# Five MLP units inside batch 1's attention chain, its features reordered, its weight loads moved

## The chip, the cores and the metric

One core of a Trainium2 chip. Its engines work side by side, each through its own list of instructions in order: TensorE (PE) does the matrix products, VectorE (DVE) and ScalarE (ACT) the elementwise work and the emptying of PSUM, GpSimd (POOL) small casts and the issue of some DMAs, SyncE (SP) the issue of the other DMAs. They wait for each other through semaphores. The metric is the device time of one execution in microseconds (us), as a median over runs.

## The reference

Eight batches of 576 rows go through an attention with a cosine weighting, without a softmax, and then through a mixer.

```python
def phi(x, c, s):
    r = np.maximum(x, 0.0)
    return np.concatenate([r * c, r * s], axis=-1)
q_p = phi(q, cos_w, sin_w)
k_p = phi(k, cos_w, sin_w)
kv = np.einsum('bhsf,bhsd->bhfd', k_p, v)
z = np.sum(k_p, axis=2)
num = np.einsum('bhsf,bhfd->bhsd', q_p, kv)
den = np.einsum('bhsf,bhf->bhs', q_p, z)[..., None] + 1e-06
...
h = xt @ U @ V
u = x + h.transpose(0, 2, 1)
ch = np.maximum(u @ w_ch1, 0.0) @ w_ch2
return (u + ch).astype(np.float32)
```

There are 8 heads of 64; x has 512 columns, U and V have rank 32, and the hidden layer of the MLP has 2048 columns. All inputs and the output are float32; the kernel multiplies in bf16.

## The kernel before

**Tiles.** A batch's 576 rows are four blocks of 128 (c = 0 to 3) and a tail of 64 (c = 4). ORD = (4, 0, 1, 2, 3) is the order in which they are mostly taken. The tails of an even and an odd batch share one tile of 128 rows.

**Attention of a batch.** q_prep and k_prep (through scaled_relu) make the features: for each block one instruction for the cosine half and one for the sine half, each on the engine that its argument names (V_ is DVE, A_ is ACT, G_ is POOL). qtr_unit transposes a block's q features on PE, eight matmuls, and an engine copies them to q_pT. v_prep and v_block cast v to bf16 in v_ext, with a column of ones. kv_unit makes k times v for four heads, and its last column is z. den_unit forms the denominators and recip their reciprocals; xh_unit forms x of one block for four heads and DVE multiplies it by the reciprocal. A_unit is x U (half the columns at a time here), uTd_open, uTd_mm and uTd_evac (uTd_close is the last two) make the transposed u for the MLP, and u_unit makes the plain u for the final addition: a product with V ("va") on PE and an addition on DVE.

**MLP.** g1_main(b, j) is one unit of the first layer: four matmuls of 512 columns with weights w_ch1, columns 128 j and on, and a ReLU by ACT into hid. g1_tail does the same for a pair's tails, g2_part the second layer and the output. The weights come through POOL's DMA queue in quarters: w1_load(n) serves j = 4n to 4n + 3, w2_load(n) the second layer.

**Order.** Everything is written out by hand. The kernel starts with batch 0's attention (chain_head, chain_mid, chain_end), where keep_warm puts matmuls on zeros between the dependent steps. Then comes a list of slots: for each pair of batches 16 units of the even batch, 16 of the odd, 4 tails, 36 parts of the second layer. After each slot what was put at its number is emitted: `at(j, ...)` for batch 1's attention, `put(...)` for the rest, and attention_plan for batches 2 to 7, whose instructions are put at numbers relative to w.

**Around the change.** Slots 0 to 6 carry batch 1's features and transposes; at slot 7 come the u units of batch 0, then chain_head(1) and chain_mid(1), with unit 8 as its only filling, at slots 9 and 10 the end of the chain. In POOL's queue a one-column copy into mark makes the following weight loads wait until the named tile has landed: before, the first two quarters of w_ch1 behind the first half of v of batch 0, the third and fourth behind the halves of v of batch 1. In SP's queue a small store, mark2, holds back the loads of batch 1 until batch 0's first reciprocals are there, and those of batch 2 until batch 1's second ones. PSUM tiles are named by tag: "g" has three buffers, "o" two, "T" and "X" one each.

Of the kernel before, what the change touches and what calls it, by code (L numbers as in the profile page):

```python
# [17 lines left out]
def kernel(  # L18
# [14 lines left out]
    H = 8  # L33
    S = 576
# [14 lines left out]
    def tail(b):  # L49
        lo = TS * (b % 2)  # L50
        return slice(lo, lo + TS)
# [49 lines left out]
    def cast(eng, o, i):  # L101
        if eng is nc.scalar:
            nc.scalar.activation(out=o, in_=i, func=AF.Copy, bias=0.0, scale=1.0)  # L103
        else:
            eng.tensor_copy(out=o, in_=i)  # L105
# [71 lines left out]
    mark2 = const.tile([1, 1], FP32)  # L177

    def cast_uv():
        cast(A_, U_bf[:, 0:4, 0:R], stU[:, 0:4, :])  # L180
        for i in range(2):
            cast(A_, U_bf[tail(i), 4 + i, 0:R], stU[tail(i), 4, :])
        cast(A_, V_bf[0:R, 0:4, :], stV[:, 0:512].rearrange("r (p c) -> r c p", c=4))
        for i in range(2):
            cast(A_, V_bf[0:R, 4, tail(i)], stV[:, 512:S])


    k_p, q_p, q_pT, kv_sb, x_bf, A_sb = {}, {}, {}, {}, {}, {}
# [2 lines left out]
    def v_prep(b, h0=0, h1=H, cs=range(5), engs=None):  # L191
        vx = v_ext[b % 2]
        for n, c in enumerate(cs):
            eng = engs[n] if engs else G_
            if eng is None:
                continue
            if c < 4:
                cast(eng, vx[:, c, h0:h1, 0:D], vst[b][:, h0:h1, c, :])
            else:
                cast(eng, vx[tail(b), 4, h0:h1, 0:D], vt[b][tail(b), h0:h1, :])  # L200

    def v_block(b, h0, h1, c0, c1, eng):
# [411 lines left out]


    TL = (0, 1, 2, 3, 4)

    def chain_head(b, warm, mid=None):
        v_prep(b, 0, 4, (4,), (A_,))
        v_block(b, 0, 4, 0, 3, V_)  # L620
        v_block(b, 0, 4, 3, 4, A_)
        if mid:
            mid()
        kv_unit(b, 0, "T", 1)
        warm(2, "o", 2)
        rec0 = den_unit(b, 0, 4, "X", 1)
        v_prep(b, 4, 8, (4,), (A_,))
        v_block(b, 4, 8, 0, 4, A_)
        warm(1, "g", 3)
        for n, c in enumerate(ORD):  # L630
            xh_unit(b, c, 0, 4, rec0, *(("o", 2) if n in (0, 1, 4) else ("g", 3)))
            if n == 3:
                kv_unit(b, 1, "T", 1, A_)
        return rec0

    def chain_mid(b, warm, fill):
        warm(1, "g", 3)
        rec1 = den_unit(b, 4, 8, "g", 3)
        if b == 1:

            nc.sync.dma_start(out=mark2, in_=rec1[0:1, 0, 0:1])
        u01 = ps.tile([P, 2, 512], FP32, tag="X", bufs=1, name="u01")
        uTd_open(b, 0, None, None, u01[:, 0, :].rearrange("p (c t) -> p c t", c=4))
        uTd_open(b, 1, None, None, u01[:, 1, :].rearrange("p (c t) -> p c t", c=4))
        a0 = A_unit(b, "T", 1, A_, 0, 256)
        for n, c in enumerate(ORD[:3]):
            xh_unit(b, c, 4, 8, rec1, *(("o", 2), ("g", 3))[n % 2])
        fill()
        uTd_mm(b, 0)
        uTd_mm(b, 1)  # L650
        uTd_evac(b, 0, A_)
        uTd_evac(b, 1, A_)
        for n, c in enumerate(ORD[3:]):
            xh_unit(b, c, 4, 8, rec1, *(("g", 3), ("o", 2))[n % 2])
        return a0

    def chain_end(b, a0):
# [1 line left out]
        uTd_open(b, 2, "o", 2)  # L659
        uTd_open(b, 3, "o", 2)  # L660

    def none(*a):
        pass

    keep_warm(22, "X", 1)
    for c in TL:
        q_prep(0, c, (V_, V_ if c == 3 else A_))
    for n, c in enumerate(TL):
        qtr_unit(0, c, 0, H, (V_, A_, V_, A_, V_)[n], "g", 3)
        keep_warm(1, "o", 2)  # L670
    for c in TL:
        k_prep(0, c, (V_, V_ if c == 3 else A_))
    keep_warm(13, "o", 2)

    def w1_begin():
        G_.tensor_copy(out=mark, in_=vst[0][0:TS, 3, 0, 0:1])
        w1_load(0)
        w1_load(1)

    rec0 = chain_head(0, keep_warm, w1_begin)  # L680
    cast_uv()

    nc.sync.dma_start(out=mark2, in_=rec0[0:1, 0, 0:1])
    alloc_q(1)
# [6 lines left out]
    load_tail(vt[1], v, 1)  # L691
    load_main(vst[1], v, 1, 0, 4)
    load_main(vst[1], v, 1, 4, 8)
    a0 = chain_mid(0, keep_warm, none)
    keep_warm(2, "g", 3)
    chain_end(0, a0)
    g1_main(0, 0, True)
    uTd_close(0, 2, V_)
# [7 lines left out]
    def at(j, *thunks):  # L706
        beside.setdefault(j, []).extend(thunks)

    for n, c in enumerate(ORD):
        at(n, lambda c=c, n=n: q_prep(1, c, (V_, A_ if n % 2 == 0 else V_)))  # L710
        ev = A_ if n == 3 else V_
        tg = ("T", 1) if n % 2 else ("o", 2)
        at(2 + n, lambda c=c, ev=ev, tg=tg: qtr_unit(1, c, eng=ev, tag=tg[0], bufs=tg[1]))
        at((3, 4, 5, 6, 6)[n], lambda c=c, n=n: k_prep(1, c, (V_, A_ if n % 2 else V_)))
    for c in ORD:
        at(7, lambda c=c: u_unit(0, c, "o", 2))

    def w1_end():
        G_.tensor_copy(out=mark, in_=vst[1][0:TS, 3, 0, 0:1])
        w1_load(2)  # L720
        G_.tensor_copy(out=mark, in_=vst[1][0:TS, 7, 0, 0:1])
        w1_load(3)
        for n in range(4):
            w2_load(n)

    at(7, lambda: chain_head(1, none, w1_end))
    st1 = {}
    at(7, lambda: st1.update(a=chain_mid(1, none, lambda: g1_main(0, 8))))
    at(9, lambda: chain_end(1, st1["a"]))
    at(10, lambda: uTd_close(1, 2, V_), lambda: uTd_close(1, 3, A_))  # L730

    slots, todo = [], {}
    for pr in range(NPAIR):
        e, o = 2 * pr, 2 * pr + 1
        slots += [
            (lambda: None) if (pr, j) == (0, 8) else lambda j=j, e=e: g1_main(e, j)
            for j in range(NJ)
        ]
        slots += [lambda j=j, o=o: g1_main(o, j) for j in range(NJ)]
        slots += [lambda j=j, pr=pr: g1_tail(pr, j) for j in range(4)]  # L740
        slots += [
            lambda cc=cc, p=p, pr=pr: g2_part(pr, cc, p) for cc in range(9) for p in range(4)
        ]
# [4 lines left out]
        todo.setdefault(at, []).append(thunk)  # L748

    put(17, lambda: uTt_direct(0, "o", 2, V_))  # L750
    for n, c in enumerate(ORD):
        put(18 + n, lambda c=c: u_unit(1, c, *spare(18)))
    for n, t in enumerate(loads(2, nc.sync)):
        put((11, 12, 12)[n], t)
    for b, w in ((2, 40), (3, 57), (4, 88), (5, 124), (6, 160), (7, 196)):
# [36 lines left out]
```

## Time and profile before

| what | value |
|---|---|
| median of 8 runs | 341.98 us (341.26 to 343.4) |
| the profiled execution | 342.84 us, span 341.1 us |
| mean granted clock of PE | 0.979 of full |
| PE busy | 322.6 us, 95% of the span |
| DVE, ACT, POOL busy | 45%, 49%, 8% |
| q, k of batch 1 (main part) issued, landed | 18.25 to 27.9 us, 20.18 to 32.7 us |
| v of batch 1, both halves landed | 35.1 and 36.1 us |
| third and fourth quarter of w_ch1 landed | 41.0 and 44.5 us |

A landing here is the start of the DMA's issue plus the time to landing that the trace gives. The span runs from the first to the last instruction; the 1.74 us between it and the execution's time lie around it. A row of the timeline gives start, duration, engine, line, instruction and, in brackets, how long the engine stood idle before it and what ended that. A row of the windows gives for each stretch the busy time of the engines, the granted clock of PE, the mean share of the DMA engines, and GB/s. "PEclk" in the page gives the clock in tenths for 40 equal slices of 8.5 us.

### The profile page before, as it was taken

What the parts mean: (1) busy time and instruction counts of PE and PEld (TensorE: products, weight loads), DVE (VectorE), ACT (ScalarE), POOL (GpSimd) and SP (SyncE); (2) the same over time, 40 slices, a digit from 0 to 9 for tenths busy, and PEclk for the clock granted to TensorE, in tenths of its full rate; (3) what the DMA queues carried; (4) which work ended last, traced back from release to release, by engine and by line L of the source; (5) the groups of instructions that cost most, each with busy time, mean ns of one, the idle gap of its engine ahead of it and who ended that gap; (6) DMA issues with size and microseconds to landing.
All of it is one profiled execution on the core that took longest, in us unless ns stands there. A gap on an engine that the chain in (4) does not pass through costs nothing.

```text
span 341.1 us, 5844 instructions
## 1 busy us (share of the span) xinstructions
PE 322.6 (95%) x2428; PEld 172.9 (51%) x2428; DVE 152.1 (45%) x334; ACT 165.5 (49%) x278; POOL 28.3 (8%) x55
## 2 busy tenths in 40 slices
PE   8996679999989979999999999999999999999995
PEld 3663275447545534455645544557445444464444
DVE  7663953381465785034553790144725630001211
ACT  4754805578671904655760376565910046660000
POOL 1200600300101010000011110000011100000000
PEclk9997958999999999999999999999999999999999
DMA  7999799946633412893259939920392140001131
GB/s 237 227 242 262 112 193 294 352 139 213 218 116 124 121 62 63 186 310 107 63 152 270 321 98 218 325 84 2 95 231 59 62 112 2 0 2 62 62 94 62
DMA packets 79054, 50.73 MB, mean 149 GB/s; under 512 B 47188, under 2 KB 76244, under 8 KB 79028
## 3 DMA queue, kind: packets, MB, share of 16 engines
q1 hardware_dynamic: 72596, 39.09, 40.5%
q0 software_dynamic: 6432, 11.27, 13.5%
q8 instruction: 19, 0.31, 0.4%
q14 instruction: 7, 0.06, 0.1%
HBM read 36.86 MB, written 9.44 MB: 136 GB/s over the span
## 4 chain that ended last, share of the span: by engine, by line
PE 64%; DVE 4%; issue 1%; ACT 1%; DVEq 0%
PE o_ps L518 29%; PE g_ps L466 24%; PE gt_ps L486 3%; PE va_ps L382 2%; PE kv_ps L245 2%; PE x_ps L339 2%; DVE k_p L213 2%; PE a_ps L365 2%; DVE o_sb L528 1%; PE t_ps L262 1%; DVE k_tl L213 1%; DVE rec L297 0%; ACT k_p L211 0%; DVE x_bf L349 0%; DVE rec L296 0%
## 5 line engine op out<-in xcount | busy, mean ns | idle before, releaser
L466 PE MATMUL g_ps<-uT,w_bf 128*128 128x512 bf16 x512 | 119.7, 384 | 0.0
L518 PE MATMUL o_ps<-w_bf,hid 128*128 128x512 bf16 (+1 forms) x528 | 118.2, 372 | 0.5 <-DVE o_sb L528 0.5
L475 ACT ACTIVATE hid<-g_ps 128x512 bf16<-128x512 f32 x128 | 76.2, 596 | 83.9 <-PE g_ps L466 83.9
L466 PEld LDWEIGHTS <-w_bf 128*128 128x128 bf16 x512 | 49.1, 99 | 55.7 <-issue 1.7
L518 PEld LDWEIGHTS <-hid 128*128 128x128 bf16 x528 | 49.9, 98 | 53.6 <-issue 1.6
L528 DVE TENSOR_TENSOR o_sb<-u_bf,o_ps 128x512 f32<-128x512 bf16 (+1 forms) x33 | 22.1, 669 | 67.8 <-PE o_ps L518 67.7
L538 POOL DMA_DIRECT2D out_dram<-o_sb x24 | 13.4, 558 | 181.6 <-DVE o_sb L528 164.5
L383 DVE TENSOR_TENSOR u_bf<-x_bf,va_ps 128x512 bf16<-128x512 bf16 x32 | 21.6, 685 | 9.0 <-PE va_ps L382 9.0
L105 DVE CAST kv<-kv_ps 128x260 bf16<-128x260 f32 x14 | 6.0, 428 | 37.7 <-PE kv_ps L245 37.7
L211 ACT ACTIVATE q_p<-qst,sinw 128x512 bf16<-128x512 f32 x29 | 20.4, 709 | 3.8 <-DMA qst<-in_q_dram 3.8
L382 PE MATMUL va_ps<-A_sb,V_bf 128*128 128x512 bf16 x40 | 15.1, 379 | 2.5 <-DVE u_tl L383 1.6
L349 DVE TENSOR_TENSOR x_bf<-x_ps,rec 128x512 bf16<-128x512 f32 x24 | 16.6, 691 | 0.8
L103 ACT ACTIVATE v_ext<-vst 128x512 bf16<-128x512 f32 (+2 forms) x24 | 15.2, 643 | 2.4 <-DMA vst<-in_v_dram 2.3
L486 PE MATMUL gt_ps<-uT_tl,w_bf 128*128 128x128 bf16 x256 | 16.1, 219 | 0.0
L486 PEld LDWEIGHTS <-w_bf 128*128 128x128 bf16 x256 | 15.1, 98 | 1.4
L518 PE MATMUL o_ps<-w_bf,hid_tl 128*128 128x512 bf16 x64 | 15.4, 379 | 0.0
L245 PEld LDWEIGHTS <-k_p 128*128 128x128 bf16 x256 | 12.0, 102 | 5.9 <-DVE v_ext L105 2.2
L172 PE MATMUL w_ps<-zero 128*128 128x512 bf16 x46 | 13.8, 437 | 1.2 <-DVE halfpi L142 1.2
L245 PE MATMUL kv_ps<-v_ext,k_p 128*128 128x65 bf16 x256 | 12.8, 199 | 1.8 <-DVE v_ext L105 1.3
L213 DVE TENSOR_SCALAR k_p<-kst,cosw 128x512 bf16<-128x512 f32 x28 | 13.4, 489 | 0.0
L262 PE MATMUL t_ps<-ident,q_p 128*128 128x128 bf16 x128 | 10.2, 225 | 3.3 <-ACT q_tlT L103 1.6
L339 PEld LDWEIGHTS <-q_pT 128*128 128x128 bf16 x192 | 9.1, 98 | 8.2 <-DVE x_bf L349 1.6
(99 smaller groups left out, 262.1 us busy)
## 6 DMA issues: line engine op xcount, KB each, us to landing
qst<-in_q_dram SPq DMA_DIRECT2D x8, 1024.0 KB, 8.5
kst<-in_k_dram SPq DMA_DIRECT2D x8, 1024.0 KB, 7.9
vst<-in_v_dram SPq DMA_DIRECT2D x6, 1024.0 KB, 9.0
out_dram<-o_sb POOLq DMA_DIRECT2D x24, 256.0 KB, 2.7
w_bf<-in_moe_w_ch_dram POOLq DMA_DIRECT2D x8, 512.0 KB, 9.0
vst<-in_v_dram SPq DMA_DIRECT2D x4, 512.0 KB, 7.0
out_dram<-o_sb SPq DMA_DIRECT2D x7, 256.0 KB, 2.3
qt<-in_q_dram SPq DMA_DIRECT2D x8, 128.0 KB, 7.9
```

Source lines behind the costliest of these rows:

```text
L211: nc.scalar.activation(out=o, in_=i, func=AF.Relu, bias=0.0, scale=w)
L213: eng.tensor_scalar(out=o, in0=i, scalar1=0.0, scalar2=w, op0=ALU.max, op1=ALU.mult)
L245: nc.tensor.matmul(out=acc[:, i, :], lhsT=k_p[b][:, c, h, :] if c < 4 else k_tl[:, h, :], rhs=vx[:, c, h, :], start=(c == 0), stop=(c == 4),)
L339: nc.tensor.matmul(out=acc[:, g, i * E : i * E + E], lhsT=qT_of(b, c, h), rhs=kv_sb[b][:, h, :], start=True, stop=True,)
L349: nc.vector.tensor_tensor(out=x_of(b, c, rows).rearrange("p (g i d) -> p g i d", g=2, d=D), in0=view[:, :, :, 0:D], in1=rec[rows].unsqueez ...
L382: nc.tensor.matmul(out=va, lhsT=V_bf[:, c, :], rhs=A_sb[b], start=True, stop=True)
L383: nc.vector.tensor_tensor(out=u_bf[b][:, c, :] if c < 4 else u_tl[b // 2][rows, :], in0=x_of(b, c, rows), in1=va[rows, :], op=ALU.add,)
L466: nc.tensor.matmul(out=g_ps.rearrange("p (c t) -> p c t", c=4), lhsT=w1_bf[:, d, j * P : j * P + P], rhs=uT[b][:, :, d, :], start=(d == 0) ...
L475: nc.scalar.activation(out=hid[b][:, j, :], in_=g_ps, func=AF.Relu, bias=0.0, scale=1.0)
L486: nc.tensor.matmul(out=g_ps[:, jj, :], lhsT=w1_bf[:, d, j * P : j * P + P], rhs=uT_tl[pr][:, d, :], start=(d == 0), stop=(d == 3),)
L518: nc.tensor.matmul(out=o[:, cols], lhsT=lhs[:, j, c * P : c * P + P], rhs=w2_bf[:, j, cols], start=(j == 0), stop=(j == NJ - 1),)
L528: nc.vector.tensor_tensor(out=o_sb[:, cols], in0=u[:, cols], in1=o[:, cols], op=ALU.add)
```

## The change

The casts of U and V go from ACT to POOL and are emitted before batch 0's chain. POOL's first mark copies from k's tail instead of v; the first quarter of w_ch1 follows it, the second comes behind the casts. The third and fourth and w_ch2 wait for batch 1's k instead of its v. Batch 1's k features come after all its q features, all with cosine on DVE and sine on ACT. Batch 0's u units move from slot 7 to slots 18 to 22, batch 1's to 23 to 27. The chain of batch 1 is emitted whole at slot 7, and units 8 to 12 are put inside it by fill1; their own slots are empty. Two x blocks instead of three come before the second group of uTd steps, and stand ahead of the opens. Batch 0's chain gets the same order with its keep-warm counts in warm0 (seven matmuls where there were six), and batch 1's first v casts go to DVE alone. The u opening of the last two columns is closed at slot 13 instead of 10. What is computed is the same.

```diff
     def cast_uv():
-        cast(A_, U_bf[:, 0:4, 0:R], stU[:, 0:4, :])
+        cast(G_, U_bf[:, 0:4, 0:R], stU[:, 0:4, :])
...
+    O2, G3 = ("o", 2), ("g", 3)
+
+    def chain_head(b, fill, xt, engs):
+        v_prep(b, 0, 4, (4,), (engs[0],))
         v_block(b, 0, 4, 0, 3, V_)
-        v_block(b, 0, 4, 3, 4, A_)
-        if mid:
-            mid()
+        v_block(b, 0, 4, 3, 4, engs[0])
         kv_unit(b, 0, "T", 1)
-        warm(2, "o", 2)
+        fill(0)
         rec0 = den_unit(b, 0, 4, "X", 1)
         v_prep(b, 4, 8, (4,), (A_,))
         v_block(b, 4, 8, 0, 4, A_)
-        warm(1, "g", 3)
+        fill(1)
         for n, c in enumerate(ORD):
-            xh_unit(b, c, 0, 4, rec0, *(("o", 2) if n in (0, 1, 4) else ("g", 3)))
+            xh_unit(b, c, 0, 4, rec0, *xt[n])
+            if n == 1:
+                fill(2)
             if n == 3:
                 kv_unit(b, 1, "T", 1, A_)
         return rec0
 
-    def chain_mid(b, warm, fill):
-        warm(1, "g", 3)
-        rec1 = den_unit(b, 4, 8, "g", 3)
+    def chain_mid(b, fill, xt, dt):
+        fill(3)
+        rec1 = den_unit(b, 4, 8, *dt)
...
+        for n, c in enumerate(ORD[:2]):
+            xh_unit(b, c, 4, 8, rec1, *xt[n])
         u01 = ps.tile([P, 2, 512], FP32, tag="X", bufs=1, name="u01")
...
         a0 = A_unit(b, "T", 1, A_, 0, 256)
-        for n, c in enumerate(ORD[:3]):
-            xh_unit(b, c, 4, 8, rec1, *(("o", 2), ("g", 3))[n % 2])
-        fill()
+        fill(4)
         uTd_mm(b, 0)
         uTd_mm(b, 1)
         uTd_evac(b, 0, A_)
         uTd_evac(b, 1, A_)
-        for n, c in enumerate(ORD[3:]):
-            xh_unit(b, c, 4, 8, rec1, *(("g", 3), ("o", 2))[n % 2])
+        for n, c in enumerate(ORD[2:]):
+            xh_unit(b, c, 4, 8, rec1, *xt[2 + n])
+        fill(5)
         return a0
...
+    def warm0(n):
+        m = (2, 1, 0, 1, 1, 2)[n]
+        if m:
+            keep_warm(m, *(O2 if n == 0 else G3))
...
-    def w1_begin():
-        G_.tensor_copy(out=mark, in_=vst[0][0:TS, 3, 0, 0:1])
-        w1_load(0)
-        w1_load(1)
-
-    rec0 = chain_head(0, keep_warm, w1_begin)
+    G_.tensor_copy(out=mark, in_=kt[0][0:TS, 0, 0:1])
+    w1_load(0)
     cast_uv()
+    rec0 = chain_head(0, warm0, (O2, O2, G3, G3, O2), (A_,))
+    w1_load(1)
...
         at(n, lambda c=c, n=n: q_prep(1, c, (V_, A_ if n % 2 == 0 else V_)))
-        ev = A_ if n == 3 else V_
-        tg = ("T", 1) if n % 2 else ("o", 2)
-        at(2 + n, lambda c=c, ev=ev, tg=tg: qtr_unit(1, c, eng=ev, tag=tg[0], bufs=tg[1]))
-        at((3, 4, 5, 6, 6)[n], lambda c=c, n=n: k_prep(1, c, (V_, A_ if n % 2 else V_)))
-    for c in ORD:
-        at(7, lambda c=c: u_unit(0, c, "o", 2))
-
-    def w1_end():
-        G_.tensor_copy(out=mark, in_=vst[1][0:TS, 3, 0, 0:1])
-        w1_load(2)
-        G_.tensor_copy(out=mark, in_=vst[1][0:TS, 7, 0, 0:1])
-        w1_load(3)
-        for n in range(4):
-            w2_load(n)
-
-    at(7, lambda: chain_head(1, none, w1_end))
+        tg = ("T", 1) if n % 2 else O2
+        at(2 + n, lambda c=c, tg=tg: qtr_unit(1, c, eng=V_, tag=tg[0], bufs=tg[1]))
+        at((6, 6, 7, 7, 7)[n], lambda c=c, n=n: k_prep(1, c, (V_, A_)))
+    at(6, lambda: G_.tensor_copy(out=mark, in_=kst[1][0:TS, 0, 0:1, 0]))
+    at(6, lambda: [w1_load(2), w1_load(3)] + [w2_load(n) for n in range(4)])
     st1 = {}
-    at(7, lambda: st1.update(a=chain_mid(1, none, lambda: g1_main(0, 8))))
-    at(9, lambda: chain_end(1, st1["a"]))
-    at(10, lambda: uTd_close(1, 2, V_), lambda: uTd_close(1, 3, A_))
+
+    def fill1(n):
+        if n > 0:
+            g1_main(0, 7 + n)
+
+    xt1 = (O2, O2, O2, O2, O2)
+    at(7, lambda: chain_head(1, fill1, xt1, (V_,)))
+    at(7, lambda: st1.update(a=chain_mid(1, fill1, xt1, ("T", 1))))
+    at(7, lambda: chain_end(1, st1["a"]))
+    at(13, lambda: uTd_close(1, 2, V_), lambda: uTd_close(1, 3, A_))
...
-            (lambda: None) if (pr, j) == (0, 8) else lambda j=j, e=e: g1_main(e, j)
+            (lambda: None) if pr == 0 and 8 <= j < 13 else lambda j=j, e=e: g1_main(e, j)
...
-    for n, c in enumerate(ORD):
-        put(18 + n, lambda c=c: u_unit(1, c, *spare(18)))
+    for n, (b, c) in enumerate([(b, c) for b in range(2) for c in ORD]):
+        put(18 + n, lambda b=b, c=c: u_unit(b, c, *spare(18)))
```

More of the change, by code (lines that the diff above doesn't have):

```diff
@@ L179, in cast_uv @@
     def cast_uv():
-        cast(A_, U_bf[:, 0:4, 0:R], stU[:, 0:4, :])
+        cast(G_, U_bf[:, 0:4, 0:R], stU[:, 0:4, :])
         for i in range(2):
-            cast(A_, U_bf[tail(i), 4 + i, 0:R], stU[tail(i), 4, :])
-        cast(A_, V_bf[0:R, 0:4, :], stV[:, 0:512].rearrange("r (p c) -> r c p", c=4))
+            cast(G_, U_bf[tail(i), 4 + i, 0:R], stU[tail(i), 4, :])
+        cast(G_, V_bf[0:R, 0:4, :], stV[:, 0:512].rearrange("r (p c) -> r c p", c=4))
         for i in range(2):
-            cast(A_, V_bf[0:R, 4, tail(i)], stV[:, 512:S])
+            cast(G_, V_bf[0:R, 4, tail(i)], stV[:, 512:S])
     k_p, q_p, q_pT, kv_sb, x_bf, A_sb = {}, {}, {}, {}, {}, {}
@@ L616 @@
     TL = (0, 1, 2, 3, 4)
-    def chain_head(b, warm, mid=None):
-        v_prep(b, 0, 4, (4,), (A_,))
+    O2, G3 = ("o", 2), ("g", 3)
+    def chain_head(b, fill, xt, engs):
+        v_prep(b, 0, 4, (4,), (engs[0],))
         v_block(b, 0, 4, 0, 3, V_)
-        v_block(b, 0, 4, 3, 4, A_)
-        if mid:
-            mid()
+        v_block(b, 0, 4, 3, 4, engs[0])
         kv_unit(b, 0, "T", 1)
-        warm(2, "o", 2)
+        fill(0)
         rec0 = den_unit(b, 0, 4, "X", 1)
@@ L660, in chain_end @@
         uTd_open(b, 3, "o", 2)
-    def none(*a):
-        pass
+    def warm0(n):
+        m = (2, 1, 0, 1, 1, 2)[n]
+        if m:
+            keep_warm(m, *(O2 if n == 0 else G3))
     keep_warm(22, "X", 1)
@@ L668 @@
     for n, c in enumerate(TL):
-        qtr_unit(0, c, 0, H, (V_, A_, V_, A_, V_)[n], "g", 3)
-        keep_warm(1, "o", 2)
+        qtr_unit(0, c, 0, H, (V_, A_, V_, A_, V_)[n], *(G3 if n < 3 else O2))
+        keep_warm(1, "X", 1)
     for c in TL:
@@ L693 @@
     load_main(vst[1], v, 1, 4, 8)
-    a0 = chain_mid(0, keep_warm, none)
-    keep_warm(2, "g", 3)
+    a0 = chain_mid(0, warm0, (O2, G3, O2, G3, O2), G3)
     chain_end(0, a0)
```

## The prediction

> **What bounds the kernel now.** I read the page first (busy shares and the 40 slices), then TensorE's timeline from 0 to 130 us, then the table of 2 us windows for the start, then the list of waits and the DMA issues with their landings, and last ScalarE's and VectorE's timelines between 26 and 46 us.
>
> ```profile
> PE 322.6 (95%) x2428; PEld 172.9 (51%) x2428; DVE 152.1 (45%) x334; ACT 165.5 (49%) x278; POOL 28.3 (8%) x55
> ...
> PEclk9997958999999999999999999999999999999999
> ```
>
> TensorE (PE) is the bound. Its granted clock is low in three slices only, all in the first 55 us, and there its busy time is inflated by the half clock. From 60 us on it stands idle for some 5 us before the last instructions. So what the change can win lies between 24 and 64 us. PE's timeline there:
>
> ```profile
> 24.03 2.32 PE L466 MATMUL g_ps<-uT,w_bf 128*128 128x512 bf16 x10
> ...
> 29.12 0.62 PE L262 MATMUL t_ps<-ident,q_tl 128*128 128x128 bf16 x8 [2.77 <-ACT q_tl L211]
> ...
> 40.95 0.38 PE L382 MATMUL va_ps<-A_sb,V_bf 128*128 128x512 bf16 x1 [1.65 <-DVE u_tl L383]
> ...
> 43.82 0.40 PE L245 MATMUL kv_ps<-v_ext,k_p 128*128 128x65 bf16 x4 [1.30 <-DVE v_ext L105]
> ...
> 57.35 6.21 PE L466 MATMUL g_ps<-uT,w_bf 128*128 128x512 bf16 x28
> ```
>
> The bracket is idle time before the row. PE waits for q of batch 1 until 29.12, starves between 38.8 and 43.8 while DVE works through its queue, and then runs the chain of batch 1 (kv at 43.82 to the last close at 57.35) with three MLP units in it. The windows show at what clock (columns: PE, PEld, DVE, ACT, POOL busy, clock, DMA share, GB/s):
>
> ```profile
> 18.00:20.00 2.00, 1.86 (x44) 1.56 (x41) 1.69 (x6) 1.74 (x5) 0.00 (x0) 1.00 1.24 207
> ...
> 30.00:32.00 2.00, 2.00 (x12) 1.16 (x11) 0.59 (x2) 1.44 (x3) 0.00 (x0) 0.50 1.07 232
> ...
> 38.00:40.00 2.00, 1.17 (x5) 0.37 (x4) 2.00 (x4) 1.74 (x4) 2.00 (x3) 1.00 1.22 205
> 40.00:42.00 2.00, 0.75 (x2) 0.19 (x2) 2.00 (x4) 1.59 (x3) 0.81 (x2) 1.00 1.11 148
> 42.00:44.00 2.00, 0.56 (x5) 0.19 (x5) 1.76 (x4) 0.00 (x0) 0.00 (x0) 0.82 1.16 172
> ...
> 46.00:48.00 2.00, 2.00 (x46) 2.00 (x44) 1.50 (x5) 0.00 (x0) 0.00 (x0) 0.50 1.22 197
> ...
> 52.00:54.00 2.00, 2.00 (x8) 0.72 (x7) 0.80 (x3) 0.28 (x1) 0.00 (x0) 0.62 1.24 207
> ```
>
> Two cold stretches: 29.7 to 33.0 after the first gap, 43.4 to 53.5 after the second. DVE is the engine at 2.00 of 2.00 in the second gap. The list of waits (total, times, longest):
>
> ```profile
> POOL mark L719 <- DMA vst<-in_v_dram: 19.8, 1, 19.8
> ...
> DVE k_tl L213 <- DMA kt<-in_k_dram: 2.5, 1, 2.5
> ```
>
> The second is DVE's strict order at work: k's tail lands at 33.06 us, and the eviction of q's transposes stands behind it; the first is what the third weight quarter waits for.
>
> [...] (29.7 to 33.0 is 3.3 us, 43.4 to 53.5 three such windows)[...] 46 to 50 us, full by the profile but with 65-column matmuls, did not restore it. [...] q of batch 1 is issued on SP at 18.25, yet the rate stays at the weights' 200 or so (the first window row above, and finer ones) until 21.0, and only then climbs to over 300. [...] Here POOL issues weights at 37.7 to 40.8 and two k features on DVE take 0.78 and 0.82 us, not 0.48; the other ones beside POOL's issues took 0.47.
>
> **The change part by part.** Prices from the trace, start to start: an MLP unit (4 matmuls) 0.86 us warm, 1.65 cold; 8 transposes 0.45 and 0.85; kv 0.60 and 1.07; den 0.50; xh 0.13; two opens 0.45 and 0.81; half an A_unit 0.54 and 1.06; two uTd_mm 0.43; a va matmul 0.21. DVE feature 0.40, ScalarE feature 0.62, hid 0.5, q_pT eviction 0.6, xh eviction 0.35 to 0.43.
>
> Start (0 to 26 us). POOL's mark waits for k's tail (some 11 us) instead of v's half (12.79), so the first weight quarter is issued 1.5 us sooner; issue to first bytes took 2.2 us before (13.07 to 15.3), so it starts at about 13.5, as v's traffic ends (13.7). Then POOL casts U and V: U's last tail lands near 15.0, six casts make about 1.7 (V's largest between POOL's 0.61 us for 128x512 and ScalarE's 1.13 for this very cast; I take 0.9), and the second quarter is issued at about 16.7 instead of 14.1, ahead of q's issue at 18.25. Its bytes run 18.9 to 21.5 (2.6 us each, as before), so q starts when it did. ScalarE loses 2.1 us of casts (18.51 to 20.5), hidden before because A_unit ended only at 20.3. Warm matmuls go from 6 to 7 in the chain of batch 0: +0.2, against the 0.23 idle at 20.92. Sum 0; bounds -0.7 (q sooner) and +1.0 (U, V or v's second half held up).
>
> q then k (26 to 40 us). PE ends its half units at 26.3 and waits for q to 29.12 as before, and is cold from 29.7 to 33.0. It then issues transposes and units in turn with nothing of k before them on DVE: transpose 29.12 to 29.57, unit to 31.2, to 32.05, unit to 33.4, then warm 33.85, 34.7, 35.15, 36.0, 36.45, and g1 unit 7 at 37.3. DVE (q 7 x 0.40, evictions 0.35 + 4 x 0.6) keeps ahead. k landed at 33.06, hidden. k's five ScalarE features are behind unit 6's and unit 7's evictions: 36.0 + 0.5 + 2 x 0.62 + 0.5 + 3 x 0.62 = 40.1, so kv starts at 40.25. DVE has k and v's first half done at about 39.5. What is late next is thus ScalarE, where before it was DVE. kv starts 3.6 us sooner: the u units (5 x 0.65 on DVE) no longer stand before v_ext, and three k features left DVE.
>
> The chain (40 to 56 us). PE was idle 37.3 to 40.25, so a second cold stretch is likely. At full clock the chain with five units, by the prices: kv 0.6, wait for its eviction 0.5, den 0.5, units 8 and 9 1.73, five xh 0.65, kv 0.6, unit 10 0.86, den 0.5, two xh and opens 0.7, A half 0.54, unit 11 0.86, uTd_mm 0.43, three xh and a wait for their two buffers 0.7, unit 12 0.86, A half and opens 1.0, unit 13 0.86, closes 0.43: 12.3 us. Cold for two windows (39.8 to 46.6, the grid of the old trace), kv ends at 41.3, den runs 42.05 to 42.6, unit 8 to 44.3, two xh and unit 9 to 46.45, and the rest warm to 55.3: 15.05. Before, the same work (units to 13 and the closes) was done at 57.35 + 3 x 0.864 = 59.94. The units' weights: the third quarter is issued at 33.3, on k's landing at 32.7, lands 5.6 us later at 38.9, and is needed at 42.6; the fourth lands near 42, needed near 52. v's traffic ended at 34.3, a microsecond before the weights' first bytes. POOL's issue of six quarters now stands beside DVE's k features: at 0.8 instead of 0.47 five of them end 1.7 us later, of which 0.7 is slack, so kv would be 1.0 late; below zero it can't go, and I take zero, as most such rows took 0.47.
>
> Moved u units. Ten, in slots 18 to 27, each 0.21 on PE beside a 0.86 unit with a 0.69 addition on DVE: five more cost +1.08. DVE then gets batch 2's features up to 4 us late; they had ended at 76.1 for transposes to 86, so that hides. Batch 2's loads start when the weights end (54.3 before, some 51 after), so DMA follows.
>
> Sum. Same cold stretches: 59.94 - 55.3 - 1.08 = 3.5 us. Without the first one PE and so kv come 1.8 us sooner; without the second 2.6: 5.4, 6.1 or 8.0. [...] I take 5.3 as the middle of the mixed cases. The profiled execution is 342.84 (span 341.1 and 1.74 around it), and so 337.5; the median of the runs, 341.98, is 0.86 lower[...]. I keep 337.5, leaving that 0.86 for stalls the walk misses.
>
> **The rivals.** (1) Warm throughout: the units inside the chain and a shorter gap keep the clock; 342.84 - 8.0 = 334.8. For it: the chain of batch 0, with warm matmuls, held 1.00. Against: two idle times of 2.8 us stay. (2) Cold through three windows as before: unit work at 1.65; another 2.5 us lost, gain 1.0, 341.8. For it: 46 to 50 us. Against: with units the array has wider matmuls. (3) Slower: the second weight quarter, now issued just ahead of q, loses the race and waits behind q, k and v, whose traffic ends at 34.3; it lands near 37.5. Unit 4 needs it at 32. PE then finishes units 4 to 7 and three transposes (4.8, plus 1.7 cold) at 44.0, k's features end at 46.4, and the chain and u units at 46.4 + 15.05 + 1.1 = 62.5, 2.6 behind: 345.4. It decides from a landing at about 34.9, where the 3.5 are gone. For it: q got no visible bytes while weights moved. Against: an output store of POOL issued at 92.36 into a load landed in 5.7 us, against 2.7 in the median, so it isn't shut out.
>
> **How the numbers follow.** Forecast (335.5 to 339.5) 0.57; warm 0.14; cold 0.13, half of it within 0.3%; slower 0.12; a hidden gain (DMA or later stages take it back) 0.04. 0.3%, about 1.0 us, is what this kernel's measurement can tell. Faster 0.77, same 0.10, slower 0.13. The range, 334.3 to 342.0, leaves out the slower case and half of the warm one.
>
> **What would show it.** kv of batch 1 near 40 us instead of 43.82, ended by ScalarE; va rows gone from 38 to 42; units 8 to 12 between kv and the closes; the last close near 53 to 55; PEclk 1.0 sooner than 53.5; third quarter issued near 33. Wrong if unit 4 waits for weights, if v lands later than 38, if the gap before kv stays near 5 us, or if the clock stays at 0.5 past 50 us.

## The result, and the profile after

The changed kernel takes 338.09 us, the median of 21 runs (336.28 to 340.21), against 341.95 for the kernel before (58 runs, 339.36 to 343.79): a ratio of 0.9891 with a 95% interval of 0.9874 to 0.9908. The forecast was 337.5. The profiled execution took 337.85 (span 336.1) against 342.84 (span 341.1).

The page of the kernel after, busy shares and the clock in 40 slices:

```profile
PE 319.5 (95%) x2429; PEld 171.2 (51%) x2429; DVE 152.5 (45%) x334; ACT 164.1 (49%) x272; POOL 29.5 (9%) x60
...
PEclk9999879999999999999999999999999999999999
```

One stretch of low clock is left where there were two (slices 5 and 6, about 39 to 46 us), 6.83 us of clock 0.50 in place of 3.41 and 10.24, and TensorE's busy time fell by 3.1 us though it runs one matmul more: what went is matmul time at half clock. The timeline of TensorE after, from 25 to 58 us (start, length, operation; in brackets the idle time ahead of it and who ended it):

```profile
25.02 2.32 PE L466 MATMUL g_ps<-uT,w_bf 128*128 128x512 bf16 x10
28.79 0.62 PE L262 MATMUL t_ps<-ident,q_tl 128*128 128x128 bf16 x8 [1.45 <-ACT q_tl L211]
...
34.49 1.03 PE L466 MATMUL g_ps<-uT,w_bf 128*128 128x512 bf16 x4
38.24 0.25 PE L245 MATMUL kv_ps<-v_ext,k_p 128*128 128x65 bf16 x3 [2.73 <-DVE v_ext L105]
38.70 0.20 PE L245 MATMUL kv_ps<-v_ext,k_p 128*128 128x65 bf16 x1 [0.21 <-ACT k_p L211]
...
40.45 1.87 PE L466 MATMUL g_ps<-uT,w_bf 128*128 128x512 bf16 x4
...
42.55 1.90 PE L466 MATMUL g_ps<-uT,w_bf 128*128 128x512 bf16 x4
...
54.10 3.62 PE L466 MATMUL g_ps<-uT,w_bf 128*128 128x512 bf16 x16
```

The wait for q is 1.45 us instead of 2.77. The va rows that stood between 38 and 42 are gone, unit 7 (the row at 34.49) is followed by a single wait of 2.73, and kv of batch 1 starts at 38.24 instead of 43.82. That wait is ended by VectorE's last cast of v; ScalarE's last k features come 0.5 later, so both engines hold kv at nearly the same time. The closes are done at 54.10; the same work (units to 13 and closes) was done at 59.94 before. The shift stays to the end: the first transposes of batch 2 stand at 72.25 instead of 77.02, 4.8 sooner, and the span is 5.0 shorter. No later stage took any of it back.

The 2 us windows of the kernel after (columns as in the prediction: busy time of PE, PEld, DVE, ACT and POOL, clock, DMA share, GB/s):

```profile
38.00:40.00 2.00, 1.03 (x24) 0.84 (x25) 0.73 (x3) 1.95 (x4) 0.00 (x0) 0.85 1.19 185
40.00:42.00 2.00, 2.00 (x24) 1.00 (x24) 0.46 (x2) 0.19 (x1) 0.00 (x0) 0.50 1.20 187
...
44.00:46.00 2.00, 2.00 (x35) 1.76 (x33) 0.76 (x2) 0.60 (x1) 0.00 (x0) 0.50 1.24 203
46.00:48.00 2.00, 2.00 (x41) 1.45 (x39) 0.73 (x3) 0.98 (x2) 0.00 (x0) 0.94 1.24 208
```

The cold stretch starts at 39.4, after the wait has ended, and lasts until 46.2. That is 6.83 us, twice the 3.41 of the first cold stretch of the kernel before; 3.41 us is called a window here. How many are lost differs from one execution to the next, and the mean clock of each says by how much: one window of 3.4 us at half clock costs 3.4 / (2 x 337) = 0.5% of it. Of 22 executions of the kernel after, ten had 0.984 (three windows, mean 339.5 us), eight 0.989 or 0.990 (two, 337.6), four 0.993 or 0.995 (about one, 336.7). So a window more or less is worth 1 to 2 us (0.9 and 1.9 between these classes), and the median of a version depends on how often it falls into each class.

### The profile page after: what moved, and what is told of

Read it like the earlier page. It is cut to its first block, busy times and chain, and to the rows that moved or that the text cites. A ratio compares the mean times of both kernels' runs of the same rounds, so it can differ in the third digit from the quotient of the medians.

```text
span 336.1 us, 5849 instructions
## 1 busy us (share of the span) xinstructions
PE 319.5 (95%) x2429; PEld 171.2 (51%) x2429; DVE 152.5 (45%) x334; ACT 164.1 (49%) x272; POOL 29.5 (9%) x60
## 4 chain that ended last, share of the span: by engine, by line
PE 65%; DVE 4%; issue 1%; ACT 1%; DVEq 0%
PE o_ps L518 30%; PE g_ps L466 25%; PE gt_ps L486 3%; PE va_ps L382 2%; PE kv_ps L245 2%; PE x_ps L339 2%; DVE k_p L213 2%; PE a_ps L365 2%; DVE o_sb L528 1%; PE t_ps L262 1%; DVE k_tl L213 1%; DVE rec L297 0%; ACT k_p L211 0%; DVE x_bf L349 0%; DVE rec L296 0%
## 5 line engine op out<-in xcount | busy, mean ns | idle before, releaser
L172 PE MATMUL w_ps<-zero 128*128 128x512 bf16 x47 | 14.1, 430 | 1.4 <-DVE halfpi L142 1.2
L296 DVE TENSOR_SCALAR rec<-x_ps 128x8 f32<-128x8 f32 (+1 forms) x30 | 4.9, 165 | 17.0 <-PE x_ps L339 16.9
```

## The experiments

Each ratio is to the kernel before, run on the same chip beside it, with its 95% interval; that kernel's medians there were 341.25, 341.03 and 341.39 in the three groups of four. The diffs are against the kernel after unless something else is said.

### What held kv: the u units on VectorE's queue

**u_back** puts batch 0's u units back ahead of batch 1's chain.

```diff
+    for c in ORD:
+        at(7, lambda c=c: u_unit(0, c, *O2))
     at(7, lambda: chain_head(1, fill1, xt1, (V_,)))
...
-    for n, (b, c) in enumerate([(b, c) for b in range(2) for c in ORD]):
-        put(18 + n, lambda b=b, c=c: u_unit(b, c, *spare(18)))
+    for n, c in enumerate(ORD):
+        put(18 + n, lambda c=c: u_unit(1, c, *spare(18)))
```

> The changed kernel with one part undone: batch 0's u units stand before batch 1's chain again. Theory (DVE's order sets the start of kv): five additions of 0.65 us stand before DVE's v casts, which end at 38.1 in the changed kernel, so kv of batch 1 starts 3.0 to 3.3 us later, near 41.5; the five va matmuls (1.08) are then paid inside the wait, so 2.0 to 2.3 us slower than the changed kernel, ratio to before 0.995 to 0.997. Rival (ScalarE's k features, which end at 38.65, hold kv anyway and hide DVE): less than 0.5 us slower, ratio 0.989 to 0.991.

Measured: 338.81 us, 0.9939 (0.9906 to 0.9972). TensorE's timeline of u_back:

```profile
36.90 0.38 PE L382 MATMUL va_ps<-A_sb,V_bf 128*128 128x512 bf16 x1 [1.53 <-DVE u_tl L383]
...
40.38 0.42 PE L245 MATMUL kv_ps<-v_ext,k_p 128*128 128x65 bf16 x4 [1.70 <-DVE v_ext L105]
```

The va rows wait again for VectorE's additions, and kv starts 5.94 us after the end of unit 7 (34.44), against 2.89 after 35.35 in the kernel after. That is 3.05 us for five additions and their va matmuls, the size that was expected for kv. The whole lost less than expected: 0.995 to 0.997 was said, and by the two ratios it is some 1.6 us slower than the kernel after instead of 2.0 to 2.3.

**only_u** is the reverse: the kernel before with nothing changed but that move.

```diff
-    for c in ORD:
-        at(7, lambda c=c: u_unit(0, c, "o", 2))
...
-    for n, c in enumerate(ORD):
-        put(18 + n, lambda c=c: u_unit(1, c, *spare(18)))
+    for n, (b, c) in enumerate([(b, c) for b in range(2) for c in ORD]):
+        put(18 + n, lambda b=b, c=c: u_unit(b, c, *spare(18)))
```

> The kernel before with one part alone: batch 0's u units moved from slot 7 to slots 18 to 22, batch 1's to 23 to 27. Theory: five additions of 0.65 us leave DVE's queue before its v cast, kv of batch 1 starts about 3 us sooner (near 40.8 on the old trace), and 1.1 us of va matmuls come later: 1.5 to 2.0 us faster than before, ratio 0.994 to 0.996. Rival (PE's wait only moves, ScalarE's v casts end at 40.1 and 41.6 anyway): ratio 0.998 to 1.000.

Measured: 337.97 us, 0.9912 (0.9877 to 0.9947), so 3.0 us by this move alone where 1.5 to 2.0 were expected. TensorE's timeline of only_u:

```profile
29.89 1.03 PE L262 MATMUL t_ps<-ident,q_tl 128*128 128x128 bf16 x8 [3.47 <-ACT q_tl L211]
...
41.16 0.30 PE L245 MATMUL kv_ps<-v_ext,k_p 128*128 128x65 bf16 x4 [2.24 <-DVE v_ext L105]
...
53.95 6.21 PE L466 MATMUL g_ps<-uT,w_bf 128*128 128x512 bf16 x28
```

Everything up to q is as in the kernel before (the wait is even 3.47), and yet kv starts at 41.16, 2.7 sooner (3.4, counted from the first transposes), and the long run of units at 53.95 instead of 57.35. Its executions spread from 0.980 to 1.000 in clock, two of eight without any cold window (336.3); in the execution shown the clock fell both after the wait for q and in the chain. This one move has most of the change's gain: 0.0088 of the 0.0109 in ratio (0.0053 to 0.0123 by its interval).

### The units inside the chain

**no_fill** takes all five out of the chain and runs them behind it; **fill3** keeps three units ahead of the closes, all late as in the kernel before: two inside the chain (8 and 9, in its last two places for a unit) and the third, unit 10, in its own slot.

```diff
     def fill1(n):
-        if n > 0:
-            g1_main(0, 7 + n)
+        if n > 3:
+            g1_main(0, 4 + n)
...
-    at(13, lambda: uTd_close(1, 2, V_), lambda: uTd_close(1, 3, A_))
+    at(10, lambda: uTd_close(1, 2, V_), lambda: uTd_close(1, 3, A_))
...
-            (lambda: None) if pr == 0 and 8 <= j < 13 else lambda j=j, e=e: g1_main(e, j)
+            (lambda: None) if pr == 0 and 8 <= j < 10 else lambda j=j, e=e: g1_main(e, j)
```

(This is fill3. In no_fill, fill1 returns at once, and slots 8 to 12 run their units.)

> The changed kernel with one part undone: no MLP unit inside batch 1's chain, units 8 to 12 run after it. Theory (the units cover waits[...]): the chain's own waits (for DVE's and ScalarE's evictions) are bare and its clock stays low, 1.0 to 3.0 us slower than the changed kernel, ratio 0.992 to 0.998; kv starts at the same 38.2. Rival (PE's work is the same, so where the units stand is without effect): within 0.5 us, ratio 0.988 to 0.991.

> The changed kernel with three units beside batch 1's chain instead of five, standing late as in the kernel before: unit 8 in the middle, unit 9 before the last A half, unit 10 before the closes. The move of the u units alone gave 0.991, the whole change 0.989, no unit at all 0.999. Theory (the first waits of the chain, at den and xh, are bare again and the clock stays low there): 0.5 to 1.5 us slower than the changed kernel, ratio 0.990 to 0.994. Rival (the first two units carry the effect): as without units, ratio 0.996 or more. Second rival (three are enough): 0.989 or less.

Measured: no_fill 340.87 us, 0.9991 (0.9972 to 1.001); fill3 338.83, 0.9909 (0.9884 to 0.9934). TensorE's timeline of no_fill:

```profile
37.43 0.40 PE L245 MATMUL kv_ps<-v_ext,k_p 128*128 128x65 bf16 x4 [3.03 <-DVE v_ext L105]
...
41.01 0.83 PE L321 MATMUL xh_ps<-kv,q_pT 128*128 128x64 bf16 x8 [0.66 <-DVE x_tl L325]
...
46.93 0.86 PE L431 MATMUL u<-V_bf,A_sb 128*128 128x512 bf16 x2 [0.48 <-ACT A_sb L103]
```

With no units the whole gain is gone, more than the 0.992 to 0.998 that was expected, although kv starts at 37.43. The chain then shows six waits (0.52, 0.66, 0.26, 0.48, 0.39, 0.19) and stays cold (clock 0.50) from 37.2 to 47.5; the executions lie between 0.973 and 0.985. But fill3, with the first group of steps bare as it was before (waits of 0.52, 0.66 and 0.26), is slower than the kernel after by 0.2% in ratio, and the intervals overlap: that units stand in the chain matters, while five instead of three can't be told from no gain. Set beside only_u, fill3 says more: it is the whole change but for where the units stand, and its 0.9909 is only_u's 0.9912. With late units, the new start, the order of q and k and the earlier weights together show no gain of their own.

### The clock

**warm_gap** fills the wait in front of kv with twelve matmuls on zeros, which are the kernel's own keep-warm; **warm4** with four.

```diff
+    at(7, lambda: keep_warm(12, "X", 1))
     at(7, lambda: chain_head(1, fill1, xt1, (V_,)))
```

> The changed kernel with twelve matmuls on zeros (2.6 us warm) put into PE's wait before kv of batch 1 (35.4 to 38.2). Theory (the wait is what makes the clock low from 39.4 to 46): the chain runs at full clock, 2.5 to 3.0 us faster where two cold windows followed, about 2 us on the median, ratio 0.982 to 0.986, mean clock 0.995 or more. Rival (the chain's own narrow matmuls make the clock fall): no gain, ratio 0.988 to 0.992, with 0.5 again behind kv.

> The changed kernel with four matmuls on zeros (0.9 us) before kv instead of twelve, so that about 2 us of the wait stay idle. Theory [...] the clock falls in some executions or none, mean clock above the changed kernel's: ratio 0.980 to 0.987. Rival (any wait of 2 us before narrow matmuls makes it fall): clock 0.984 to 0.990 as without zeros, ratio 0.988 or more.

Measured: warm_gap 333.77 us, 0.9802 (0.9757 to 0.9846), somewhat more than was expected; warm4 335.39, 0.9811 (0.9767 to 0.9856), as its theory had it. The timeline of warm_gap, and its windows:

```profile
33.88 2.75 PE L172 MATMUL w_ps<-zero 128*128 128x512 bf16 x12
...
38.44 0.54 PE L304 MATMUL d_ps<-kv,q_pT 128*128 128x1 bf16 x16 [0.52 <-DVE kv L105]
...
49.90 3.62 PE L466 MATMUL g_ps<-uT,w_bf 128*128 128x512 bf16 x16
```

```profile
42.00:44.00 2.00, 2.00 (x44) 1.53 (x41) 0.88 (x3) 0.97 (x2) 0.00 (x0) 1.00 1.24 204
```

The clock is 1.000 in five of six executions, and the closes are done 11.5 us after den starts (14.2 in the kernel after). By the ratios that is 3.0 us below the kernel after (4.3 between the medians, but the kernel before ran 0.7 faster beside warm_gap), by work that computes nothing. With four zeros a wait of 2.17 stays:

```profile
37.01 0.36 PE L245 MATMUL kv_ps<-v_ext,k_p 128*128 128x65 bf16 x4 [2.17 <-DVE v_ext L105]
```

(TensorE's timeline of warm4.) Its profiled execution was at full clock, like one other (mean 333.7); the other four had 0.990 to 0.994 and took 335.2 to 336.5. So with four zeros it differs from one execution to the next whether a window is lost; what decides it isn't shown.

**no_fill_warm** joins no_fill and the twelve zeros, to see whether the units do more than keep the clock.

```diff
     def fill1(n):
-        if n > 0:
-            g1_main(0, 7 + n)
+        return
...
+    at(7, lambda: keep_warm(12, "X", 1))
```

> Units 8 to 12 out of batch 1's chain, as in the run without them, and twelve matmuls on zeros in the wait before kv, as in the run with them. If the units were worth 3.4 us because they keep the clock up, the zeros do that too: clock 0.995 or more and ratio near 0.986, half or more of the loss gone. If they were worth it because they cover the chain's own waits, most of the 3.4 us stays: ratio 0.989 or more against the 0.980 of the run with zeros and units. If the chain's narrow matmuls make the clock fall whatever stands before it: 0.5 within the chain again, ratio 0.995 or more.

Measured: 338.9 us, 0.994 (0.9915 to 0.9966). Windows of no_fill_warm:

```profile
42.00:44.00 2.00, 1.65 (x40) 1.55 (x37) 1.06 (x4) 0.39 (x1) 0.00 (x0) 0.59 1.23 201
44.00:46.00 2.00, 1.56 (x10) 0.89 (x8) 0.68 (x2) 0.38 (x1) 0.00 (x0) 0.50 1.24 208
```

Zeros in front of kv don't save a chain without units: it idles 2.7 us in six pieces, the longest 0.85, and the clock falls in the middle of it, at 42.3. The row to compare is that of warm_gap above, with 2.00 busy and 1.00. Units are thus worth 338.9 - 333.8 = 5.1 us once the gap is filled (4.7 by the ratios), by covering the chain's short waits and by keeping its clock. How much is covering and how much is clock this run doesn't part: 0.994 is what was expected where units cover waits (0.989 or more), and its interval reaches into what was expected where the narrow matmuls alone take the clock down (0.995 or more).

**before_warm** puts zeros into the kernel before, seven behind its second and seven behind its fifth u unit.

```diff
     for n, c in enumerate(ORD):
         at(7, lambda c=c: u_unit(0, c, "o", 2))
+        if n in (1, 4):
+            at(7, lambda: keep_warm(7, "X", 1))
```

> The kernel before with twice seven matmuls on zeros in PE's waits between batch 0's u units and before kv of batch 1. If the change's gain were the clock's alone, this would give it too: ratio 0.989 or less. Theory (the u units on DVE hold kv, and three late units don't keep the chain's clock): kv stays near 43.8, the clock falls later or for fewer windows: 1 to 2.5 us faster, ratio 0.993 to 0.997, and at least 9 us above the changed kernel with zeros is not made up.

Measured: 338.75 us, 0.9921 (0.99 to 0.9942); its executions at 0.999 take 337.59. TensorE's timeline of before_warm:

```profile
41.57 0.29 PE L245 MATMUL kv_ps<-v_ext,k_p 128*128 128x65 bf16 x4
...
42.86 0.54 PE L304 MATMUL d_ps<-kv,q_pT 128*128 128x1 bf16 x16 [0.52 <-DVE kv L105]
...
51.98 6.21 PE L466 MATMUL g_ps<-uT,w_bf 128*128 128x512 bf16 x28
```

Zeros alone bring the old kernel 2.6 us, two thirds of what the whole change brings, and a little more than was expected; kv starts at 41.57 and not near 43.8, mostly because q came 1.5 us sooner in this execution. At full clock on both sides 337.6 against 333.8 remain: den starts at 42.86 here and at 38.44 in warm_gap. So the change isn't the clock's alone: with the clock full in both kernels the earlier and denser chain is still worth 3.8 us. The 9 us that were expected to remain between this run and warm_gap are 5.0.

### The order of q and k

**k_mixed** puts batch 1's k features between its q features again, on their old engines.

```diff
-        at((6, 6, 7, 7, 7)[n], lambda c=c, n=n: k_prep(1, c, (V_, A_)))
+        at((3, 4, 5, 6, 6)[n], lambda c=c, n=n: k_prep(1, c, (V_, A_ if n % 2 else V_)))
```

> The changed kernel with one part undone: batch 1's k features between the q features, three of ten back from ScalarE to DVE. Theory: DVE meets k's tail before it has landed (31.7) with evictions of q behind it, so PE's transposes stall, and DVE has 1.2 us more before its v casts: kv 1 to 2 us later, ratio 0.992 to 0.996. Rival (only the total before kv counts, and ScalarE is relieved by what DVE gets): within 0.5 us, ratio 0.988 to 0.991.

Measured: 338.18 us, 0.991 (0.988 to 0.9941), against 0.9891 for the change. TensorE's timeline of k_mixed:

```profile
33.79 0.62 PE L262 MATMUL t_ps<-ident,q_p 128*128 128x128 bf16 x8 [2.18 <-DVE q_p L213]
...
39.61 0.39 PE L245 MATMUL kv_ps<-v_ext,k_p 128*128 128x65 bf16 x4 [2.54 <-DVE v_ext L105]
```

The old order brings a wait of 2.18 inside the q phase, for a q feature that stands on VectorE behind one of k; kv comes at 39.61 instead of 38.24. Counted from the first transposes, which stand at 27.50 here and at 28.79 there, that is 12.11 against 9.45, so 2.7 us later and more than the 1 to 2 expected. But the idle time is now in two pieces 5.8 us apart, and four of its eight executions lose one window only (0.993 or 0.994). The ratios differ by 0.2%, less than kv's delay and less than the intervals can tell: the trace bears out the theory, the time the rival.

### The weights

**w_late** lets the third and fourth quarter wait for v again, as before.

```diff
-    at(6, lambda: G_.tensor_copy(out=mark, in_=kst[1][0:TS, 0, 0:1, 0]))
-    at(6, lambda: [w1_load(2), w1_load(3)] + [w2_load(n) for n in range(4)])
+    at(6, lambda: G_.tensor_copy(out=mark, in_=vst[1][0:TS, 3, 0, 0:1]))
+    at(6, lambda: w1_load(2))
+    at(6, lambda: G_.tensor_copy(out=mark, in_=vst[1][0:TS, 7, 0, 0:1]))
+    at(6, lambda: [w1_load(3)] + [w2_load(n) for n in range(4)])
```

> The changed kernel with one part undone: the third and fourth quarter of w_ch1 wait for the halves of batch 1's v again. Theory (the early weights only make the units possible, and have slack): the third quarter lands near 40, unit 8 wants it at 40.4, so at most 0.5 us slower than the changed kernel, ratio 0.988 to 0.992. Rival (the weights' place in the DMA order is where the gain comes from): 1.5 us slower or more, ratio 0.994 or more, with a wait of PE before unit 8.

Measured: 337.14 us, 0.9885 (0.9859 to 0.9911): no loss. The third quarter is issued at 33.10, on v's landing, and unit 8 starts at 39.84 without a wait for it. The earlier mark buys nothing at this place.

**warm_tail** is warm_gap with q's tail loaded ahead of its main part (the line of load_main, not shown, stands between), to see whether the wait for q's tail holds kv.

```diff
+    load_tail(qt[1], q, 1)
...
-    load_tail(qt[1], q, 1)
```

> The changed kernel with the twelve matmuls on zeros before kv, and q's tail of batch 1 loaded ahead of its main part. In the changed kernel the main part landed at 24.2 and the tail, which the first transposes want, at 28.0, with the second weight quarter in between. Theory: both land near 25, PE's wait of 1.2 to 1.5 us before the first transposes goes, and kv comes up to 1.2 us sooner: ratio 0.976 to 0.979. Rival (k's landing holds kv): as without it, 0.980.

Measured: 333.89 us, 0.9786 (0.9757 to 0.9815). The tail landed by 25.3, but this execution issued its loads of q from 18.37 on, 0.8 us later than that of warm_gap, and PE was done with its half units 0.8 later too. So PE's wait fell from 1.24 to 0.57, but the first transposes stand at 27.49 (27.32 in warm_gap) and kv at 37.02 (36.78). The ratio lies in the theory's range, and the interval holds the rival's 0.980 as well: the run doesn't settle what holds kv. In every profile with this order kv follows the first transposes by 9.4 to 9.8 us, though k landed at 29.6 in warm_gap and at 31.2 here, which speaks against the rival.

**w1_pair** issues the second quarter right behind the first, ahead of POOL's casts.

```diff
     w1_load(0)
+    w1_load(1)
     cast_uv()
     rec0 = chain_head(0, warm0, (O2, O2, G3, G3, O2), (A_,))
-    w1_load(1)
```

> The changed kernel with one part undone: the second quarter of w_ch1 right behind the first, before POOL's casts. In the changed kernel it was issued at 18.8, beside q of batch 1, and its bytes ran from 23.5 to 26.0 between those of q's main part and q's tail. Theory: with it out of the way by 19 or 20, q's bytes run without a break; q's tail lands 0 to 2 us sooner, k's landing (the last of the same bytes) stays, and so does the time: ratio 0.987 to 0.991. Rival (the place of the second quarter matters): 1.0 us or more either way.

Measured: 334.92 us, 0.9812 (0.9769 to 0.9855); 0.987 to 0.991 was expected by the theory, and the rival that gave the second quarter's place a price is right: 2.7 us below the kernel after by the ratios. First POOL's timeline in the kernel after, then POOL's and TensorE's in w1_pair:

```profile
16.63 0.71 POOL L105 CAST U_bf<-st_uv 128x128 bf16<-128x128 f32 x3 [2.18 <-DMA st_uv<-in_moe_U_dram]
17.40 1.47 POOL L105 CAST V_bf<-st_uv 32x512 bf16<-32x512 f32 x3
18.82 0.78 POOL L91 DMA_DIRECT2D w_bf<-in_moe_w_ch_dram  x1
```

```profile
10.47 1.87 POOL L91 DMA_DIRECT2D w_bf<-in_moe_w_ch_dram  x2
```

```profile
26.70 0.62 PE L262 MATMUL t_ps<-ident,q_tl 128*128 128x128 bf16 x8 [0.57 <-ACT q_tl L211]
...
36.15 0.25 PE L245 MATMUL kv_ps<-v_ext,k_p 128*128 128x65 bf16 x3 [2.72 <-DVE v_ext L105]
...
50.90 3.62 PE L466 MATMUL g_ps<-uT,w_bf 128*128 128x512 bf16 x16
```

In the kernel after, the casts hold POOL until 18.8, and the second quarter is issued in the same moment as q (18.79 on SP). In half-microsecond windows of it (TensorE's busy time, clock, DMA share, GB/s) one sees where its bytes go:

```profile
22.50:23.00 0.50, 0.50 (x7) 1.00 1.06 369
...
23.50:24.00 0.50, 0.50 (x8) 1.00 1.29 227
...
24.50:25.00 0.50, 0.50 (x4) 1.00 1.19 195
...
27.00:27.50 0.50, 0.34 (x2) 1.00 1.09 379
```

From 23.5 to 26.0 the rate drops from 369 to the 200 or so of a weight load: most of the quarter moves between q's main part (landed 24.2) and its tail (28.0). The packets of the two queues (q0 is POOL's, q1 SP's) show how they share, from 24.5 to 26.0 in this execution and from 21.5 to 24.5 in that of w_late:

```profile
q0 software_dynamic: 229, 0.23, 91.9%
q1 hardware_dynamic: 201, 0.05, 26.0%
```

```profile
q0 software_dynamic: 355, 0.36, 71.0%
q1 hardware_dynamic: 401, 0.37, 45.4%
```

(A line gives packets, MB and the time that they took as a share of all 16 engines.) The queues sent packets in nearly equal numbers in both stretches; SP's are small in the first (0.05 MB in 201), so that few of the bytes are SP's. In w1_pair nearly all bytes of both quarters are through by 18.6, and q's tail lands 6.2 us after its issue, at 24.3, where it took 8.7 in the kernel after. To compare kv, executions are needed in which q is issued at the same time, for k of batch 0 landed later in the one of the kernel after: w1_pair (q at 17.58) has kv at 36.15, warm_gap (17.53) at 36.78, w_late (17.59) at 37.27. So kv comes 0.6 to 1.1 sooner, and the executions lose one window (0.993, 0.994) or two (0.988), none of them three. At equal clock w1_pair still takes some 2.0 us less than the kernel after (334.8 against 336.7 in the class of one window, 335.5 against 337.6 in that of two); 0.6 of that the kernel before, too, was faster beside w1_pair. So about half of the 2.7 us is there at equal clock, and the rest is fewer cold windows. Together with zeros in front of kv it was not tried.

## Why the prediction was right

The direction and nearly the size came out, and most of the mechanism; in one place, the wait for q, luck helped. A change of -5.3 was forecast for the profiled execution, and -5.0 was measured; the medians lie 3.9 apart, because the execution of before that served as the base was 0.9 above its own median and that of after 0.2 below. By the steps:

- **The u units.** Right. They stood on VectorE ahead of v, and u_back gives them 3.05 us at kv. That they cost +1.08 where they went is right as well: 59.94 - 54.10 less 1.08 is 4.76, and batch 2's first transposes are 4.77 sooner.
- **q then k.** From the first transposes to kv the walk is right: 28.79 to 38.24 is 9.45 us (9.39 to 9.76 in the eight other profiles with this order and without u units in it), and the forecast's 11.13 had 1.8 of half clock in it, which leaves 9.3. The wait for q was off: 2.77 "as before" was taken, and 1.45 came, because batch 0's chain ended 1.0 later in this execution (its k landed at 12.1 instead of 10.6, before any changed instruction runs) and q's tail landed 0.3 sooner. So the first cold stretch is gone, the case that was given 5.4. That this case came is luck as far as the prediction goes, which left it open, and it isn't shown to be the change's doing: with the changed start the wait is 0.57 to 1.74 in ten more profiles, and in none does the clock fall there; with the old start it is 2.77 and 3.47 where the clock fell, but 0.57 in before_warm, where it stayed up. kv is not ended by ScalarE, as forecast, but by both: VectorE's v_ext ends the wait of 2.73, ScalarE's k_p another 0.21. Beside POOL's issues from 31.3 to 35.9 three of five features on VectorE took 0.56 to 0.71 us instead of 0.48, 0.45 us in all, where the forecast had set its 1.0 to zero; of the rows that it read, the one at 37.27 had taken 0.61 too. The order of q and k by itself had no price in the sum, and k_mixed shows little.
- **The chain.** 15.05 was forecast, 38.24 to 54.10 is 15.86. Up to unit 9 the walk holds (6.0 us against 6.2). Then the three xh groups and the second kv from 44.24 to 46.0 still ran at half clock, as it lasted until 46.24, 8.0 us after kv's start, where the forecast had 6.35 (46.6 for a kv at 40.25): 0.8 us. With kv 0.16 ahead of its case this makes 54.10 where that case gives 53.5.
- **The cold windows.** That their number is open was said, with none and three among the rivals, and it differs from one execution to the next: 10 of 22 executions lose three windows. So what the second rival feared, given 13%, is in part the same outcome, and at 339.5 us instead of 341.8. Whether the three windows of such an execution include a stretch before kv isn't known, since the one timeline that was kept has two. The reading that 46 to 50 us of the kernel before were full is off (48 to 50 is 1.74 of 2.00 busy); what this says of the clock stands in the last section.
- **Weights at k's landing.** Issued at 31.26, forecast 33.3; no unit waited. By w_late this part is worth nothing, which the sum had too.
- **The start.** The profiled execution left the forecast here: "the second quarter is issued at about 16.7 instead of 14.1, ahead of q's issue at 18.25", and q was to start when it did. The casts began at 16.63, since U landed late, and took 2.2 us for 1.7; the quarter was issued at 18.82, behind q, and its bytes went into the middle of batch 1's loads. It landed at 27.7 and unit 4 didn't wait, so the third rival (a landing after 34.9) didn't come. In the nine other profiles with this order on POOL the quarter was issued 0.1 to 1.4 us ahead of q, as forecast, and in warm_gap (16.29) its bytes ran from 19.0 to 21.0 and q's behind them. So against the kernel before the sum of nothing isn't shown to be wrong. What it didn't see is that the place in front of the casts is better: by w1_pair it is worth about 2.7 us (0.9812 against 0.9891, intervals apart only by 0.0019).

What isn't shown: when two queues share and when one goes first, and where a window begins in an execution. Whether the six executions of w1_pair lose fewer windows because of the quarter's place, or by chance, stays open. The casts on POOL, the first mark and batch 0's new order were not run alone.

## What to carry to other kernels

Work that nobody waits for, on the in-order queue of an engine that the next chain waits for, is the first thing to move: one such move by itself brought 0.0088 of the 0.0109 here. Then fill the wait that stays, with useful tiles inside the chain and, where there are none, with zeros: twelve matmuls on zeros in a gap of 2.7 us brought another 3.0 us. When a load is moved behind a cast, follow its bytes in several executions and not only its issue in one: 1.24 us ahead of q's issue they ran in front of q, 0.03 behind it they ran in the middle of q.

## What the runs showed of the hardware

- A load of POOL and the loads of SP shared the engines in more than one way. In the kernel after (24.5 to 26.0) and in w_late (21.5 to 24.5) both queues sent packets in nearly equal numbers, 229 to 201 and 355 to 401; with small packets SP's load got 0.05 MB beside 0.23. In warm_gap, where the weights were issued 1.24 us ahead of q, POOL's queue sent 400 packets from 19.0 to 21.0 and SP's none, at 196 to 214 GB/s, though q had been issued at 17.53. What decides between the two isn't shown.
- Busy time by the profile alone didn't tell when the clock comes back. In the kernel before it was low for 3.41 us, full for 10.24 and low for 10.24, in the kernel after low for 6.83: one, three, three and two times 3.41, so windows of 3.41 can be marked off from where the clock fell. In the kernel before the one from 46.70 to 50.11, busy for 3.15 us with kv, den, xh and transposes (65, 1, 64 and 128 columns), ended cold; in no_fill_warm the one from 45.76 to 49.17, busy for 2.83 us with opens, xh and x U (512, 64 and 256 columns), ended with the clock back. In the kernel after a window that was busy throughout (42.83 to 46.24), half of it with 64 and 65 columns, ended with the clock back as well. That the width counts is the author's reading of these three windows, and isn't shown. With zeros of 128x512 in the gap the clock stayed at 1.000 in five of six executions of warm_gap; in the kernel after, without them, in none of 22.
- What a wait does to the clock, and when, differed from one execution to the next. In the kernel after a wait of 2.73 ended at 38.24 and the clock fell at 39.4, while one of 1.45, which ended at 28.79, was followed by 1.00 until then; in no_fill the clock fell at 37.2, before the wait of 3.03 ended at 37.43. In warm4 the profiled execution had a wait of 2.17 and a clock of 1.000, and four of the six executions had 0.990 to 0.994.
- In no_fill_warm the clock fell at 42.3 without a long wait just ahead of it: the 3.41 us before were busy for 2.20, with no idle piece over 0.85.
